# A gated mix of a long convolution and a shifted MLP: x added to the second product by accumulating DMAs, two small jobs moved, and a finer ranking of the planner's work

## Chip, cores and metric

The kernel runs on one core of a Trainium2 chip. The metric is the device time of the whole program in microseconds. The core's engines are TensorE (PE; its weight loads are PEld), VectorE (DVE), ScalarE (ACT), GpSimd (POOL) and SyncE (SP). Here POOL mostly issues DMAs, among them all DMAs that add to their destination; SP issues plain DMAs and transposing ones.

## What is computed

S = 2048 tokens of D = 640, bfloat16; the MLP has F = 1536. The reference, cut to what matters:

```python
def A(q, k, v, shift_k, ssm_k, ssm_D):
    k_shift = sum(k_pad[:, t:t + S, :] * shift_k[:, 3 - t] for t in range(4))
    kv = k_shift * v
    y = irfft(rfft(kv, 2 * S) * rfft(ssm_k, 2 * S))[:S]      # long causal convolution
    return q * (y + kv * ssm_D)

def B(x, w1, w2, w3, w4):
    h = gelu(layernorm(x) @ w1)
    hs = shift_quarters(h, (+1, -1, +2, -2)) @ w2            # token shifts by quarter of D
    x1 = x + hs
    return x1 + gelu(layernorm(x1) @ w3) @ w4

x = A_q
g = sigmoid((x * gate_w).sum(-1))
out = g * A(x, ...) + (1 - g) * B(x, ...)
```

## The kernel before

**Tiles.** Token s = 1024 c + 8 p + rho sits on partition p, in one of 2 halves c and 8 rows rho. X (bfloat16, all 16 tiles of 128 x 640) holds x, then x1, then the output. XT holds the transposed layernorm, HT the first product's result, KV the product of shifted k and v. Five slots s0 to s4 of 5120 elements a partition, and two more in the taps' place, hold the transforms.

**MLP.** First layernorm by rows (0), (1), (2, 3), (4, 5), (6, 7): statistics on VectorE (`ln_bn`) or, for row 1, on ScalarE; the inverse root on POOL (L661); the scaling on VectorE (L705); transposes on TensorE (L718). First product (L794) in 4 stages of two rows; its results go through gelu to HT. HT has two pad columns, set to zero at L779, which overlay the row with the shift taps that TensorE reads at L589. 32 columns of each quarter go through `w1t`, a copy of parts of w1 that POOL makes (L565). Second product (L840) in 4 groups of two rows, two halves each, so 16 products, and each of them adds x by one more matmul with the identity per half (L843); ScalarE evicts the sum back into X (L511, tag `x1`). The second layernorm takes its statistics on VectorE for groups 0 and 1 (`LN2_DVE`) and on ScalarE for groups 2 and 3, scales on VectorE and is transposed by DMAs on SP. The load of w3's second half waits for the last second product and the first transposes, the loads of w4 for those transposes. Third and fourth products (L883, L902) follow in 4 stages.

**Convolution.** The transform is cut into 4 units (two halves of D, two residues kap). A unit takes forward transforms of the taps h and of kv (L938), a butterfly of each (`bh`, `bk`), a window, a pointwise complex product and a fold, all of these by `tt` (L484) on VectorE; then come inverse transforms on TensorE (L1099). The pointwise product has two forms: `pointwise`, and `pointwise_dma`, in which two of the sums are accumulating DMAs on POOL (`accumulate`, L522, tags `pwa` and `pwb`). `PW_DMA` lists the units (half, kap) with the second form. Slot s4 is the temporary of every unit's butterflies, pointwise product and fold.

**Order.** The program is a list of nodes with costs and dependences. `schedule` and `_forward` place them one at a time: of all nodes that are ready, the one that can start first on its engine comes next, and among equals the one of higher rank. Ranks are looked up by a node's tag, and the tag has its stage behind a colon (`mm2:4` is the second product's first group). The planner's clock decides nothing on the chip: there each engine runs its list in that fixed order and waits on semaphores. A dependence through memory follows from the order in which the nodes are written down; the second product is written down ahead of all units.

`MM2_DMA`, empty before, lists the groups of the second product in which x isn't added by matmuls: such a product is evicted to a staging place in slot s4 (four rows of it, used in turn), and when both halves of a row are there, `accumulate` adds them to X (tag `add2`). The mean of such rows is the mean of the product plus that of x (`ln_small`, L666).

Of the kernel before, what the change touches and what calls it, by code (L numbers as in the profile page):

```python
# [10 lines left out]
ACTF = mybir.ActivationFunctionType  # L11
# [68 lines left out]
class Prog:  # L80
# [66 lines left out]

    def schedule(self):

        for n in self.nodes:  # L150
            n.base = frozenset(n.deps)
            for d in n.deps:
                d.users.append(n)
        for n in reversed(self.nodes):
            tail = max((u.prio for u in n.users), default=0.0)
            n.prio = tail + (n.cost if n.kind == "c" else n.cost + 2.0 + n.bytes / self.RATE)
        for n in self.nodes:
            n.prio = self.PRIO.get(n.tag, n.prio)
        self._forward()

    def _forward(self):
# [10 lines left out]
        known_at = {}  # L172
        pair_free = [0.0] * PAIRS
        pair_job = [None] * PAIRS
        link = 1.6
        xlink = 0.0

        def move(at, nbytes):
# [20 lines left out]
        while left:  # L199
# [16 lines left out]
            n = best[1]  # L216
            e = n.eng
# [6 lines left out]
            elif n.kind == "dma" and e == "pool" and n.bytes < self.SMALL:  # L224
                link = move(link, n.bytes)
                n.end = t + 4.5
            elif n.kind == "dma":
                link = move(max(link, t), n.bytes)
# [132 lines left out]
def bass_gated_mix__ssm_conv_h3__mixer_s_mlp__prompt_kernel(  # L361
# [4 lines left out]
    LN1_XP = ()  # L366
    SUM_DMA = (0,)
    KV_DMA = ((1, 0), (1, 1))
    MM2_DMA = ()
    W_AFTER = True  # L370
    PW_NEG = ()
    BF_DMA = ()
    INV_SPLIT = ((1, 0), (1, 4))
    PW_DMA = ((0, 0), (0, 1), (1, 0))
    LN1_ROWS = ((0,), (1,), (2, 3), (4, 5), (6, 7))
    LN1_DVE, LN2_DVE = ((0,), (2, 3), (4, 5), (6, 7)), (0, 1)
    P = Prog(nc)
# [51 lines left out]
    w1t = V(oW12 + 3200, 640).rearrange("p (c f) -> p c f", c=5)  # L429
# [4 lines left out]
    GM = V(oGM, 4096).rearrange("p (a i r s k) -> p a i r s k", a=2, i=2, r=4, s=2)  # L434
# [9 lines left out]
    ident = V(oID, 128)  # L444
# [35 lines left out]
    def dve(fn, r, w, n, psum=False, tag="", **kw):  # L480
        return P.op("dve", lambda e, ps: fn(e), r=r, w=w, cost=c_dve(n, psum), tag=tag, **kw)
# [4 lines left out]
    def act(o, i, func, n, scale=None, bias=None, acc=None, tag="", group=None, job=None, accgroup=None):  # L486
        r = [x for x in (i, scale, bias) if x is not None and not isinstance(x, float)]
        kw = {}
        if scale is not None:
            kw["scale"] = scale  # L490
        if bias is not None:
            kw["bias"] = bias
        if acc is not None:
            kw["accum_out"] = acc
        naps = sum(1 for x in (scale, bias) if x is not None and not isinstance(x, float))
        node = P.op("act", lambda e, ps: e.activation(o, i, func, **kw), r=r, w=[o], cost=c_act(n, naps, acc is not None),  # L496
                    tag=tag, group=group)
        if acc is not None:
            P._track(node, [], [acc], accgroup)
        return node  # L500
# [58 lines left out]
    for c in range(2):  # L559
# [2 lines left out]
    load_halo(0)  # L562
    load_k(0, 0)
    w1s, w1d = w1v.rearrange("p c (g f) -> p c g f", g=4)[:, :, :, 128:160], w1t.rearrange("p c (g f) -> p c g f", g=4)
    P.op("pool", lambda e, ps: e.tensor_copy(w1d, w1s), r=[w1s], w=[w1d], cost=1.2, tag="w1t")  # L565
    load_k(0, 1)
    load_x("sp", 0, 4, 8)
    load_x("sp", 1, 4, 8)
# [3 lines left out]
          w=[GWT], nbytes=100000, after=[late], tag="gw")  # L572
# [184 lines left out]
    v0, r0, nm0 = [stat(0, f)[:, :, 0:2] for f in ("var", "rs", "nm")]  # L757
# [18 lines left out]
    SHIFT = [1, -1, 2, -2]  # L776
    for col in (0, 257):
        z = HT[:, 0:4, :, col:col + 1]
        dve(lambda e, z=z: e.memset(z, 0.0), [], [z], 32, group="pad")  # L779
    for j, d0 in enumerate(SHIFT):  # L780
        rs = slice(0, d0) if d0 > 0 else slice(8 + d0, 8)
        col = 1 if d0 > 0 else 256
        z = HT[32 * j:32 * j + 32, 4, rs, col:col + 1]
        dve(lambda e, z=z: e.memset(z, 0.0), [], [z], 2, group="tail")
    RAW = [V(oGM + 512 * i, 512) for i in range(2)]
    for sc in range(4):
        P.stage = sc
        for fp in range(3):
# [13 lines left out]
            else:  # L802
                raw = RAW[sc % 2]
                evict(job, raw, lambda ps: bank(ps, 0, 512), ACTF.Gelu_apprx_tanh, 512, tag="gelu1t")
                for j, d0 in enumerate(SHIFT):
# [4 lines left out]
                    for carry, lst in todo.items():  # L810
                        k0, rho0, n = lst[0][0], lst[0][1], len(lst)
# [275 lines left out]
    def inverse(half, slot0, slot1):  # L1087
# [50 lines left out]
    inverse(1, "s3", "k0")  # L1138

    P.PRIO = {  # L1140
# [25 lines left out]
    }  # L1166
    P.schedule()
    P.assign_waits()
# [30 lines left out]
```

## Time and profile before

| | us |
|---|---|
| three runs, median (lowest to highest) | 244.91 (243.86 to 245.47) |
| profiled execution | 245.85 |
| its span, first to last instruction | 244.1 |
| mean granted TensorE clock | 0.987 |

The span lies inside the profiled execution's time. Busy times in microseconds, by stretches of the span:

```profile
core 0: us, PE busy (x) PEld busy (x) DVE busy (x) ACT busy (x) POOL busy (x), PEclk, DMA share, GB/s
0.00:20.00 20.00, 9.82 (x42) 4.67 (x43) 15.15 (x60) 10.05 (x17) 6.59 (x14) 1.00 0.93 335
20.00:40.00 20.00, 19.84 (x178) 12.98 (x180) 18.57 (x35) 17.35 (x18) 7.47 (x12) 1.00 1.03 358
40.00:60.00 20.00, 19.95 (x209) 13.71 (x209) 17.69 (x17) 14.23 (x21) 8.48 (x13) 0.91 0.63 154
60.00:80.00 20.00, 20.00 (x149) 14.43 (x148) 19.90 (x39) 13.14 (x25) 3.39 (x3) 1.00 0.41 74
80.00:100.00 20.00, 19.95 (x135) 13.15 (x135) 14.60 (x25) 19.51 (x35) 2.86 (x4) 1.00 0.75 165
```

PEclk is the granted share of TensorE's clock, and the DMA share is that of the core's 16 DMA engines. A busy time counts overlapping instructions once; a group's mean duration contains the overlap with its neighbours. In the chain of waits each line is a start, a length and what the end of the program depended on there.

### The profile page before, as it was taken

The numbers are of one execution on the slowest core, as the hardware profiler recorded it, in microseconds if no ns is written. First come the engines' busy times: TensorE is split into PE (matmuls) and PEld (weight loads), VectorE is DVE, ScalarE is ACT, GpSimd is POOL, SyncE is SP. The second block draws the span as 40 slices with busy tenths as digits, with TensorE's granted clock in tenths as the row PEclk, the third lists the DMA queues.
The fourth block names the chain that finished last, engine by engine and source line by source line (L and its number), as shares of the span: only waits on it lengthen the run. The fifth ranks groups of instructions, "written<-read, shape, count | busy, mean of one in ns | idle before, by whom it ended". The sixth has DMA issues, their size and how long they took to land.

```text
span 244.1 us, 3961 instructions
## 1 busy us (share of the span) xinstructions
PE 223.6 (92%) x1557; PEld 142.4 (58%) x1569; DVE 215.7 (88%) x337; ACT 154.3 (63%) x236; POOL 57.9 (24%) x70
## 2 busy tenths in 40 slices
PE   0579999999999999969999999999999998999990
PEld 0236576577777775525677645577546773777760
DVE  4899989996999758998989699799994899999992
ACT  5536899647468999956997456652257224127881
POOL 5311452451013040145002121001220011015910
PEclk9999999979999999999999999999999999999997
DMA  6999998098019649665585325403248034934998
GB/s 217 369 398 331 397 362 301 22 246 156 3 19 191 88 113 293 141 129 107 106 104 183 56 51 77 85 3 54 53 56 110 0 55 70 382 88 74 160 214 253
DMA packets 29938, 37.32 MB, mean 153 GB/s; under 512 B 12464, under 2 KB 22960, under 8 KB 29792
## 3 DMA queue, kind: packets, MB, share of 16 engines
q0 software_dynamic: 9424, 15.21, 32.0%
q1 hardware_dynamic: 20496, 21.86, 29.7%
q8 instruction: 12, 0.20, 0.3%
q14 instruction: 6, 0.05, 0.1%
HBM read 21.79 MB, written 2.62 MB: 100 GB/s over the span
## 4 chain that ended last, share of the span: by engine, by line
PE 88%; DMA 5%; DVE 3%; ACT 1%; issue 1%; SPq 0%; ACTq 0%
PE PS L902 21%; PE PS L883 18%; PE PS L938 14%; PE PS L794 10%; PE PS L840 9%; PE PS L1099 7%; DMA arena<-in_B_w_dram 3%; PE PS L641 3%; PE PS L718 2%; PE PS L843 2%; DMA arena<-in_A_q_dram 1%; DVE arena L686 1%; ACT arena L511 1%; PE PS L752 1%; DVE arena L705 1%
## 5 line engine op out<-in xcount | busy, mean ns | idle before, releaser
L484 DVE TENSOR_TENSOR arena<-arena 128x1280 bf16<-128x1280 bf16 (+2 forms) x192 | 180.3, 999 | 12.3 <-ACT arena L511 9.9
L511 ACT ACTIVATE arena<-PS 128x640 bf16<-128x640 f32 (+3 forms) x129 | 96.6, 821 | 42.5 <-PE PS L883 21.9
L522 POOL DMA_DIRECT2D arena<-arena x26 | 29.4, 1207 | 106.3 <-ACT arena L511 64.8
L883 PE MATMUL PS<-arena 128*128 128x512 bf16 x232 | 51.9, 379 | 2.4 <-DMA arena<-in_B_w_dram 2.0
L902 PE MATMUL PS<-arena 128*128 128x320 bf16 x384 | 52.8, 299 | 1.1 <-ACT arena L511 1.1
L511 ACT ACTIVATE arena<-PS,arena 128x320 bf16<-128x320 f32 (+1 forms) x48 | 27.6, 615 | 36.9 <-PE PS L902 34.2
L902 PEld LDWEIGHTS PS<-arena 128*128 128x128 bf16 x384 | 37.5, 98 | 16.1 <-ACT arena L511 1.6
L883 PEld LDWEIGHTS PS<-arena 128*128 128x128 bf16 x240 | 23.3, 98 | 29.6 <-DMA arena<-in_B_w_dram 2.5
L938 PE MATMUL PS<-arena 128*128 128x320 bf16 x256 | 36.4, 299 | 0.0
L938 PEld LDWEIGHTS PS<-arena 128*128 128x128 bf16 x256 | 25.1, 98 | 10.6
L840 PE MATMUL PS<-arena 128*128 128x320 bf16 x160 | 27.6, 310 | 0.0
L794 PE MATMUL PS<-arena 128*128 128x512 bf16 x96 | 23.8, 404 | 1.6 <-ACT arena L511 1.4
L686 DVE BATCH_NORM_STATS2 arena<-arena 128x6 f32<-128x320 bf16 x44 | 19.0, 467 | 4.9 <-DMA arena<-in_A_q_dram 2.5
L496 ACT ACTIVATE arena<-arena 128x640 bf16<-128x640 bf16 (+2 forms) x30 | 21.8, 756 | 1.7 <-DMA arena<-in_A_q_dram 1.7
L840 PEld LDWEIGHTS PS<-arena 128*128 128x128 bf16 x160 | 16.1, 101 | 6.8
L794 PEld LDWEIGHTS PS<-arena 128*128 128x128 bf16 x100 | 10.0, 103 | 13.6 <-issue 4.4
L1099 PE MATMUL PS<-arena 128*128 128x320 bf16 x128 | 17.6, 299 | 0.0
L1099 PEld LDWEIGHTS PS<-arena 128*128 128x128 bf16 x128 | 12.5, 98 | 4.9
L661 POOL TENSOR_TENSOR arena<-arena 128x4 f32<-128x4 f32 (+1 forms) x9 | 10.1, 1118 | 16.7 <-DVE arena L691 11.4
L705 DVE TENSOR_SCALAR arena<-arena 128x640 bf16<-128x640 bf16 x32 | 12.4, 440 | 1.3 <-issue 1.2
L822 POOL DMA_DIRECT2D arena<-arena x18 | 9.7, 544 | 8.5 <-ACT arena L511 8.5
L645 ACT ACTIVATE arena<-PS 128x1280 bf16<-128x1280 bf16 x8 | 9.5, 1263 | 2.4 <-PE PS L641 2.4
(43 smaller groups left out, 73.3 us busy)
## 6 DMA issues: line engine op xcount, KB each, us to landing
arena<-arena POOLq DMA_DIRECT2D x7, 640.0 KB, 5.6
arena<-in_A_q_dram SPq DMA_DIRECT2D x6, 640.0 KB, 8.0
arena<-in_B_w_dram POOLq DMA_DIRECT2D x4, 960.0 KB, 7.7
arena<-arena POOLq DMA_DIRECT2D x11, 320.0 KB, 3.7
arena<-in_A_ssm_k_dram SPq DMA_DIRECT2D x5, 512.0 KB, 11.4
arena<-in_A_k_dram SPq DMA_DIRECT2D x4, 640.0 KB, 17.1
arena<-in_A_v_dram SPq DMA_DIRECT2D x4, 640.0 KB, 20.5
out_dram<-arena SPq DMA_DIRECT2D x16, 160.0 KB, 2.1
```

Of the source, the lines that this page charges most:

```text
L484: return dve(lambda e: e.tensor_tensor(o, a, b, op), [a, b], [o], n, tag=tag, **kw)
L496: node = P.op("act", lambda e, ps: e.activation(o, i, func, **kw), r=r, w=[o], cost=c_act(n, naps, acc is not None), tag=tag, group=group)
L511: node = P.op("act", lambda e, ps: e.activation(ov, inner(ps), func, **kw), r=r, w=[o], cost=c_act(n, len(r), acc is not None), job=job, t ...
L522: P.dma("pool", lambda e, ps: e.dma_start(o, i, accum_op=ALU.add, max_dma_last_dim=2560), r=[o, i], w=[o], nbytes=3 * 256 * n, cost=1.2, t ...
L686: dve(lambda e, o=o, x=x: e.bn_stats(o, x), [x], [o], 640, tag="bn", group=("bn", l, rho, c))
L705: P.op("dve", lambda e, ps, b=b, x=x, rs=rs, nb=nb: e.tensor_scalar(b, x, rs, nb, op0=ALU.mult, op1=ALU.add), r=[x, rs, nb], w=[b], cost=0 ...
L794: fns.append(lambda e, ps, b=b, c=c, lhsT=lhsT, sc=sc: e.matmul(bank(ps, b, 512), lhsT, XT[:, c, 2 * sc:2 * sc + 2, :], start=(c == 0), st ...
L840: fns.append(lambda e, ps, hh=hh, ft=ft, lhsT=lhsT, last=by_dma and ft == 4: e.matmul(bank(ps, hh, 320), lhsT, w2v[:, ft, 320 * hh:320 * h ...
L883: fns.append(lambda e, ps, b=b, ft=ft, c=c, sc=sc: e.matmul(bank(ps, b, 512), w3v[ft // 6][:, c, 128 * (ft % 6):128 * (ft % 6) + 128], XT[ ...
L902: fns.append(lambda e, ps, hh=hh, ft=ft, lhsT=lhsT: e.matmul(bank(ps, hh, 320), lhsT, w4v[:, ft, 320 * hh:320 * hh + 320], start=(ft == 0) ...
L938: fns.append(lambda e, ps, r=r, ri=ri, s=s, b=b, rhs=rhs: e.matmul(bank(ps, b, 320), FM[:, kap, r, s, ri, :], rhs, start=(s == 0), stop=(s ...
L1099: fns.append(lambda e, ps, kap=kap, ri=ri, c=c, r=r, s=s: e.matmul(bank(ps, c, 320), GM[:, kap, ri, r, s, :], Qs[kap][:, r, ri, c, :], sta ...
```

## The change

- `MM2_DMA` names all four groups: the 32 matmuls with the identity are left out, the 16 products go to the staging place in slot s4, and 8 accumulating DMAs on POOL add them to X, one per row.
- `PW_DMA` gets the last unit (1, 1), whose pointwise product so takes the form with two accumulating DMAs.
- The copy to `w1t` moves from POOL to ScalarE.
- The memsets of the pads get a tag of their own, so that they can be ranked; they stay on VectorE.
- Tags with several nodes are cut into up to four parts (`mm2:4` becomes `mm2:4.0` to `mm2:4.3`), and the table of ranks is a new one with a rank for each part.
- The planner's start value for the DMA link goes from 1.6 to 0.8.

```diff
+        parts = {}
         for n in self.nodes:
-            n.prio = self.PRIO.get(n.tag, n.prio)
+            parts.setdefault(n.tag, []).append(n)
+        for tag, ns in parts.items():
+            for i, n in enumerate(ns):
+                if len(ns) > 1:
+                    n.tag = f"{tag}.{i * min(len(ns), 4) // len(ns)}"
+                n.prio = self.PRIO.get(n.tag, self.PRIO.get(tag, n.prio))
...
-        link = 1.6
+        link = 0.8
...
-    MM2_DMA = ()
+    MM2_DMA = (0, 1, 2, 3)
...
-    PW_DMA = ((0, 0), (0, 1), (1, 0))
+    PW_DMA = ((0, 0), (0, 1), (1, 0), (1, 1))
...
-    P.op("pool", lambda e, ps: e.tensor_copy(w1d, w1s), r=[w1s], w=[w1d], cost=1.2, tag="w1t")
+    act(w1d, w1s, ACTF.Copy, 640, tag="w1t")
...
-        dve(lambda e, z=z: e.memset(z, 0.0), [], [z], 32, group="pad")
+        dve(lambda e, z=z: e.memset(z, 0.0), [], [z], 32, group="pad", tag="pad")
...
-        dve(lambda e, z=z: e.memset(z, 0.0), [], [z], 2, group="tail")
+        dve(lambda e, z=z: e.memset(z, 0.0), [], [z], 2, group="tail", tag="pad")
...
     P.PRIO = {
...
+        "mm2:5.2": 296, "mm2:6.1": 294, "mm2:7.0": 292, "fwdh:0.3": 269, "mm2:4.2": 264, "mm2:7.1": 242,
+        "mm2:6.2": 240, "fwdh:1.2": 182, "mm2:5.3": 181, "fwdh:1.0": 179, "fwdh:0.0": 177, "mm2:4.3": 177,
+        "mm2:7.2": 177, "mm2:4.0": 159, "mm2:5.1": 159, "fwdh:1.3": 159, "fwdh:1.1": 155, "mm2:4.1": 145,
+        "fwdh:0.1": 119, "mm2:7.3": 117, "mm2:5.0": 116, "mm2:6.0": 115, "fwdh:2.0": 113, "mm2:6.3": 112,
+        "fwdh:0.2": 96, "xn:0.1": 108, "xn:0.0": 59, "pad.0": 40,
...
     }
```

The ranks shown are those of the second product, of the taps' transforms in units 0 to 2 and of the pads; the rest of the table is left out.

113 rows, old and new, of the table final are left out of this document.

## The prediction

> **What bounds the kernel now.** I read the busy shares first, then the engines by stretch, then the chain of waits in order of time, then groups by shape and VectorE's timeline. Busy shares, as busy us (share of the span) xinstructions:
>
> ```profile
> PE 223.6 (92%) x1557; PEld 142.4 (58%) x1569; DVE 215.7 (88%) x337; ACT 154.3 (63%) x236; POOL 57.9 (24%) x70
> ```
>
> Two engines are nearly full. The stretches show that it is the same ones all the way:
>
> ```profile
> core 0: us, PE busy (x) PEld busy (x) DVE busy (x) ACT busy (x) POOL busy (x), PEclk, DMA share, GB/s
> 126.00:190.00 64.00, 63.79 (x393) 38.58 (x395) 56.68 (x61) 35.21 (x46) 9.42 (x9) 1.00 0.40 72
> 190.00:223.00 33.00, 31.83 (x223) 21.60 (x223) 32.53 (x36) 9.98 (x14) 3.45 (x4) 1.00 0.40 112
> ```
>
> TensorE has no room in the first, VectorE none in the second. So a gain on TensorE alone moves the end only as far as VectorE follows. The chain (start us, us, what):
>
> ```profile
> 8.57 0.07 DVE arena L662
> 8.63 1.14 issue
> 9.78 0.15 DVE arena L705
> ...
> 10.57 0.59 DVE arena L662
> ...
> 15.05 6.45 PE PS L794 x20
> ...
> 73.04 0.68 PE PS L840 x5
> 73.72 0.14 PE PS L843
> ...
> 99.94 8.15 DMA arena<-in_B_w_dram
> ...
> 205.86 1.03 ACT arena L511
> ```
>
> To be seen: a start on VectorE with a hole of 1.14 us; then TensorE, where each half of a second product is five matmuls in 0.68 us (0.136 each) and one more in 0.14, the one that adds x; a load behind which TensorE stood 2.0 us at 106.1; a wait of 1.1 us at 205.8. Shapes, as busy us, mean ns | idle before:
>
> ```profile
> L484 DVE TENSOR_TENSOR arena<-arena 128x2560 bf16<-128x2560 bf16 x65 | 94.1, 1486 | 2.5 <-ACT arena L511 2.3
> L484 DVE TENSOR_TENSOR arena<-arena 128x1280 bf16<-128x1280 bf16 x101 | 78.0, 821 | 9.2 <-ACT arena L511 7.3 <-DMA arena<-arena 1.4
> L843 PE MATMUL PS<-arena 128*128 128x320 bf16 x32 | 9.8, 306 | 0.0
> ```
>
> The means overlap: start to start the VectorE ones are 1.41 and 0.74 us in the timeline, and L843 0.137. VectorE's timeline, and the accumulating DMAs of L522 (duration ns of the issue, then landing):
>
> ```profile
> 59.02 10.04 DVE L484 TENSOR_TENSOR arena<-arena 128x2560 bf16<-128x2560 bf16 x9 [2.27 <-ACT arena L511]
> 93.33 7.55 DVE L484 TENSOR_TENSOR arena<-arena 128x1280 bf16<-128x1280 bf16 x8 [0.99 <-ACT arena L511]
> 189.82 2.30 DVE L484 TENSOR_TENSOR arena<-arena 128x1280 bf16<-128x1280 bf16 x3 [3.67 <-ACT arena L511]
> DMA to landing us min/median/max: 3.3/4.4/7.2
> ```
>
> By the emitted order, unit 0's butterfly of h (six operations, 5.8 us by pitch) lies in the first, its window and butterfly of k (1.6 and 5.9) in the second, and its pointwise starts at 100.9.
>
> **Term 1, x by DMA: TensorE.** 32 matmuls of L843 go: 32 x 0.137 = 4.4 us (the page's chain gives this kernel's L843 2% of the span). All of it is on the chain. The same x1 evictions stay (0.70 us each).
>
> **Term 2, what x by DMA adds.** Eight accumulations of 320 KB on POOL: 8 x 1.2 = 9.8 us of a queue that is busy 3.4 of 20 us from 60 to 80, and 3.7 us from issue to landing by the 320 KB row. Behind them wait the second layernorm, its transposes, and with these the loads of w3's second half and of w4, all later in their row's chain by some 4.6 us. Cover: VectorE has the rest of k*v, TensorE the forward transforms (128 matmuls, 17.4 us). Product, transforms and half clock end near 90; the first half of w3 then covers 6.4 us. The load behind which TensorE stands now needs the last product (near 81 below) and the first transposes, so with 8.15 us it lands by 90: the 2.0 us stall goes. If that cover fails, 2.0 us stay. The Trainium skill, SBUF — State Buffer, section Who interferes with whom, says that a DMA issued from POOL cannot get its descriptors written while VectorE runs a two-port operation such as tensor_scalar, though tensor_tensor does not do this. The layernorm's four tensor_scalars in a row (0.36 us pitch) would by it hold one issue 1.5 us, and the forecast would be up to 1.5 us higher; the issues here (0.86 to 1.69 us) lie beside tensor_tensor and don't show it.
>
> **Term 3, the staging place.** The sums are staged in slot s4, which is also the temporary of every butterfly. Now unit 0's butterfly of h runs at 59 to 66, among the second products. With the change it has to wait until the last accumulation has read s4: call that R. First product at 50.4 (less the start's gain, 1.2) = 49.2; 16 x 1.36 = 21.8; the stretch at half clock now costs 1.4; so 72.4 with nothing between, and eviction 0.7 plus issue and landing 3.8 make R = 77. Each transform put before the last product adds its time, at most 17.4: R = 94.4. The new ranks place unit 2's transforms of h behind the products (they also need all of unit 0's and 1's, whose lowest rank is 96, against 112 for the lowest product), so I take the 64 matmuls of units 0 and 1 (8.7 us): R = 86. The butterflies of h and k then follow, 11.7 us: pointwise at 97.7 against 100.9, a gain of 3.2 that has the start's in it. VectorE has enough to do until R: from 24.4 to 100.9 it works 67.1 us (76.5 less 9.4 idle), without the butterflies 55.4, so it is done by 78 and idles about 8 us, as now.
>
> **Term 4, the start.** The two pads (L779) stand ahead of the first row's L705 and wait for the shift taps' matmuls, which end at 9.66: 1.15 us idle, 0.2 for the pads. At 10.49 an L662 takes 0.67 us beside POOL's copy of w1 (10.42, 0.72 us); its kind has 0.15. Removed: up to 1.9 us. The copy on ScalarE is one more ACTIVATE of 640 (0.79) in front of, at worst, the first row's eviction (1.24); the second row's then ends near 13.7 in place of 14.9. I take 1.2, ends 0 and 1.9. The pads stay on VectorE; only rank moves them.
>
> **Term 5, last unit.** Pointwise goes from six 2560s and eight 1280s to five and seven: 1.41 + 0.74 = 2.15 us off VectorE. Added: two accumulations, the larger 640 KB. In unit 2 that one started 8.9 us after its pointwise did and by its row lands 5.6 later, 7.2 at worst: 14.5 to 16.1, while VectorE has 11.7 of pointwise and 1.5 of fold. A wait of 1.3 to 2.9, into which inverse 0's multiplications (0.41 pitch, seven there now) can go. Net between 0 and 2.15 gained; I take 1.5, as units 0 to 2 show one wait on a DMA, 1.38.
>
> **Term 6, ranks by quarters, link.** They add no work; they decide who goes first. After 101 VectorE idles 9.5 us in all, 6.4 in three waits for evicted transforms (0.73, 1.96, 3.67). Bounds: 9.5 gained, or as much again lost; I take 1.5, part of the 3.67, where the window (1.6 us) needs only that its transforms come sooner.
>
> **Sum.** TensorE's path: 1.2 + 4.4 + 2.0 + 1.1 (205.8) = 8.7. VectorE's: 3.2 + 1.5 + 1.5 = 6.2. The smaller counts: 6.2. The profiled execution took 245.85 (span 244.1 and 1.75 around it): 239.65. It stands 0.94 above the median 244.91, where the same gain gives 238.7.
>
> **Rivals.** *A, both paths give way* (8.7): 236.2. For it: the waits left on VectorE mostly end on transforms, which come earlier. Against: 190 to 223 shows VectorE full. Chance 0.12.
>
> *B, VectorE keeps the end.* TensorE's 4.4 turns into waits, the staging eats what the ranks give, only the start is seen: 243.7. For it: VectorE's 88%. Against: it loses 2.15 us itself. Chance 0.15. If even the pads stay ahead, the change fails to do what it says there and this becomes 244.4.
>
> *C, slower: the staging place comes free too late.* If the last products stay behind all 128 transforms and the 19 matmuls of w3 (4.3 us) that precede them now, R = 98.7; pointwise starts at 110.4, 9.5 late; less 1.5 and 1.5, +6.5: 251.4. It decides from R = 92.2 (100.9 + 3.0 - 11.7). For it: that is the order of now, the last product ending at 99.65. Against: the ranks. Chance 0.13.
>
> **How the numbers follow.** Forecast 0.60, A 0.12, B 0.15, C 0.13. One per cent, about what a measurement here tells from no change, is 242.5 to 247.4. The forecast's own range is 236.5 to 242 (R from 80 to 89, term 5's ends). The range leaves out C and a tip of A: 235.3 to 244.3. Faster: 0.58 of the forecast + 0.12 of A + 0.03 of B = 0.73. Same: 0.02 of the forecast + 0.11 of B + 0.01 of C = 0.14. Slower: 0.01 of B + 0.12 of C = 0.13.
>
> **What would show it.** No L843; TensorE's first L794 near 13.8; no wait for w3; the last x accumulation landing near 86 and VectorE's first 2560 butterfly there; pointwise of unit 0 near 98; the last fold some 6 us sooner. It is wrong if TensorE shows new holes between 60 and 110, or if VectorE idles over 10 us before R.

## The result and the profile after

| us | median (lowest to highest), runs | ratio to before, 95% |
|---|---|---|
| before | 243.82 (241.4 to 245.47), 14 | |
| after | 246.19 (244.02 to 247.93), 14 | 1.0107 (1.0072 to 1.0143) |

The change makes the kernel about 1% slower; forecast were 238.7 and a gain. Medians and ranges, here and below, are of all runs, while the ratios leave out slow ones (over 1.5% above the kernel's fastest), without which the medians are 246.06 for after and, of the variants below, 244.76 for start_order, 241.44 for w4_late, 241.40 for both_orders and 238.58 for both_orders_half. The profiled executions mislead if they are set side by side: that of before (245.85, span 244.1) is slower than all 14 runs, that of after (244.88, span 243.1) the second fastest, and by them alone the change gains 1 us. So the lines below are read for what happens inside the program, and a second profile of each kernel stands beside them further on.

The profile after, first the busy shares (busy us, share of the span, instructions):

```profile
PE 219.9 (90%) x1537; PEld 138.7 (57%) x1537; DVE 213.6 (88%) x335; ACT 155.0 (64%) x237; POOL 71.8 (30%) x79
```

TensorE lost 3.7 us of work and two points of its share: it waits more than before. VectorE lost 2.1 us, as many as term 5 takes off it. POOL gained 13.9 us. The stretches:

```profile
core 0: us, PE busy (x) PEld busy (x) DVE busy (x) ACT busy (x) POOL busy (x), PEclk, DMA share, GB/s
72.00:90.00 18.00, 16.59 (x125) 11.48 (x124) 12.94 (x37) 16.95 (x34) 5.85 (x6) 1.00 1.14 157
96.00:100.00 4.00, 0.18 (x2) 0.05 (x2) 4.00 (x6) 2.24 (x5) 0.00 (x0) 0.98 1.04 348
100.00:103.00 3.00, 3.00 (x8) 1.07 (x9) 3.00 (x6) 0.00 (x0) 1.31 (x1) 0.50 0.54 176
126.00:190.00 64.00, 64.00 (x403) 39.18 (x402) 60.16 (x65) 39.22 (x54) 9.47 (x9) 1.00 0.40 71
190.00:223.00 33.00, 31.88 (x224) 21.63 (x222) 30.41 (x34) 11.35 (x17) 7.84 (x8) 1.00 0.67 149
```

The first of these stretches in the profile of before:

```profile
72.00:90.00 18.00, 18.00 (x135) 12.94 (x134) 14.22 (x39) 17.12 (x30) 4.55 (x6) 1.00 0.71 115
```

From 72 to 90 the DMA engines are full: the share is 1.14, before 0.71. (It is the sum of the packets' times over 16 engines; it can pass 1 only where packets overlap on an engine.) From 96 to 100 TensorE stands, and from 100 to 103 it works at half its clock. In 190 to 223 VectorE, full in the profile of before, has 2.6 us to spare. The chain (start us, us, what):

```profile
4.57 1.67 DVE arena L693 x4
...
10.81 1.26 PE PS L725 x10
...
14.52 5.07 PE PS L801 x15
...
73.80 1.18 POOL arena L529
...
79.76 2.27 SPq L719
...
82.07 7.19 DMA arena<-arena
...
89.88 0.87 POOL arena L525
90.75 9.16 DMA arena<-in_B_w_dram
...
99.96 14.73 PE PS L890 x60
...
204.15 1.03 ACT arena L518
```

The lines of the functions have moved by 7: L801 is the first product, L847 the second, L890 the third, L945 the forward transforms, L712 the scaling, L719 the second layernorm's transposes, L525 the loads, L529 the accumulations, L491 VectorE's arithmetic. To be seen: at the start VectorE's hole of 1.14 us is gone, and the first product begins at 14.52, half a microsecond sooner; an accumulation of x (73.80) and a transpose that takes 7.19 us (82.07) have come into the chain; behind it starts the load of w3's second half (90.75), which lands at 99.91; the 60 matmuls that waited for it then take 14.73 us. The wait at 204.15 is the old one of 205.86. TensorE's timeline (start, length, line; in brackets the idle time before it and what ended it):

```profile
80.79 7.30 PE L945 MATMUL PS<-arena 128*128 128x320 bf16 x52
89.50 6.64 PE L890 MATMUL PS<-arena 128*128 128x512 bf16 x30 [1.41 <-ACT arena L518]
99.96 14.73 PE L890 MATMUL PS<-arena 128*128 128x512 bf16 x60 [3.82 <-DMA arena<-in_B_w_dram]
```

The two holes add up to 5.2 us. The profile of before has one, of 2.0:

```profile
108.14 6.65 PE L883 MATMUL PS<-arena 128*128 128x512 bf16 x29 [2.03 <-DMA arena<-in_B_w_dram]
```

The first hole of after is put down to an eviction, but TensorE goes on 0.24 us after the last of the first four transposes lands (89.26), which is what the third product reads. VectorE's shapes and timeline, then the landings of L529 and of L719 (two answers about their lines):

```profile
L491 DVE TENSOR_TENSOR arena<-arena 128x2560 bf16<-128x2560 bf16 x64 | 92.3, 1482 | 3.8 <-DMA arena<-arena 3.7
L491 DVE TENSOR_TENSOR arena<-arena 128x1280 bf16<-128x1280 bf16 x100 | 76.8, 819 | 6.0 <-ACT arena L518 4.6 <-DMA arena<-arena 0.9
```

```profile
89.28 0.45 DVE L712 TENSOR_SCALAR arena<-arena 128x640 bf16<-128x640 bf16 x1 [3.13 <-DMA arena<-arena]
89.65 8.82 DVE L491 TENSOR_TENSOR arena<-arena 128x2560 bf16<-128x2560 bf16 x9
127.99 3.63 DVE L491 TENSOR_TENSOR arena<-arena 128x1280 bf16<-128x1280 bf16 x3 [3.95 <-ACT arena L518]
```

```profile
DMA to landing us min/median/max: 3.4/5.0/7.7
```

```profile
DMA to landing us min/median/max: 2.6/3.8/12.0
```

One operation of each size went. VectorE stands 3.13 us ahead of a scaling whose buffer a slow transpose is still reading, and 3.95 us ahead of a window whose transforms TensorE, late by then, has yet to do. The accumulations' median of 5.0 was 4.4; the transposes' median was 3.0 and their longest 6.3.

**Where the time went.** Issue to landing, in us, of the DMAs that decide, read from the trace's records (`xT:4` are the four transposes of the first second-layernorm group, in their order; `add2` the last two accumulations of x):

| kernel | last two `add2` | `xT:4` | w3's second half: issued, landed | took |
|---|---|---|---|---|
| before | none | 4.48, 3.66, 3.19, 2.66 | 99.94, 108.09 | 8.15 |
| after | 4.91, 6.42 | 4.87, 4.05, 5.80, 7.19 | 90.75, 99.91 | 9.16 |

The accumulations were issued at 80.05 and 82.26, the third and fourth transposes at 79.76 and 82.07. POOL stands from 83.5 to 89.9, until the transposes have landed, and then issues three of 960 KB each within 1.8 us: w4, w3's second half, w4.

### The profile page after: what moved, and what is told of

It is laid out like the page before. It is cut to its first block, busy times and chain, and to the rows that moved or that the text cites. A ratio compares the mean times of both kernels' runs of the same rounds, so it can differ in the third digit from the quotient of the medians.

```text
span 243.1 us, 3923 instructions
## 1 busy us (share of the span) xinstructions
PE 219.9 (90%) x1537; PEld 138.7 (57%) x1537; DVE 213.6 (88%) x335; ACT 155.0 (64%) x237; POOL 71.8 (30%) x79
## 4 chain that ended last, share of the span: by engine, by line
PE 80%; DMA 8%; DVE 4%; ACT 2%; POOL 1%; SPq 1%; issue 1%; ACTq 0%; POOLq 0%
PE PS L909 22%; PE PS L890 19%; PE PS L801 10%; PE PS L945 9%; PE PS L847 8%; PE PS L1106 7%; DMA arena<-in_B_w_dram 4%; DMA arena<-arena 3%; PE PS L648 2%; DVE arena L693 2%; ACT arena L518 2%; PE PS L725 2%; DMA arena<-in_A_q_dram 1%; SPq L719 1%; DVE arena L712 1%; PE PS L759 1%
## 5 line engine op out<-in xcount | busy, mean ns | idle before, releaser
L491 DVE TENSOR_TENSOR arena<-arena 128x1280 bf16<-128x1280 bf16 (+3 forms) x190 | 177.9, 995 | 12.7 <-ACT arena L518 7.0
L529 POOL DMA_DIRECT2D arena<-arena x36 | 41.9, 1201 | 106.9 <-ACT arena L518 57.8
L890 PE MATMUL PS<-arena 128*128 128x512 bf16 x240 | 54.7, 387 | 5.2 <-DMA arena<-in_B_w_dram 3.8
L909 PE MATMUL PS<-arena 128*128 128x320 bf16 x384 | 53.5, 299 | 1.1 <-ACT arena L518 1.1
L890 PEld LDWEIGHTS PS<-arena 128*128 128x128 bf16 x240 | 23.7, 99 | 34.2 <-DMA arena<-in_B_w_dram 4.3
L945 PE MATMUL PS<-arena 128*128 128x320 bf16 x256 | 37.0, 299 | 0.0
L945 PEld LDWEIGHTS PS<-arena 128*128 128x128 bf16 x256 | 24.8, 98 | 10.5 <-issue 0.2
L801 PE MATMUL PS<-arena 128*128 128x512 bf16 x100 | 24.2, 399 | 1.4 <-ACT arena L518 1.4
L847 PE MATMUL PS<-arena 128*128 128x320 bf16 x160 | 23.3, 299 | 0.0
L847 PEld LDWEIGHTS PS<-arena 128*128 128x128 bf16 x160 | 15.4, 98 | 6.1 <-DMA arena<-arena 0.3
L668 POOL TENSOR_TENSOR arena<-arena 128x4 f32<-128x4 f32 (+1 forms) x9 | 12.9, 1428 | 17.9 <-DVE arena L681 10.9
L1106 PE MATMUL PS<-arena 128*128 128x320 bf16 x128 | 17.7, 299 | 0.0
L801 PEld LDWEIGHTS PS<-arena 128*128 128x128 bf16 x100 | 9.9, 102 | 13.3 <-issue 2.2
L712 DVE TENSOR_SCALAR arena<-arena 128x640 bf16<-128x640 bf16 x32 | 12.6, 437 | 3.2 <-DMA arena<-arena 3.1
L829 POOL DMA_DIRECT2D arena<-arena x18 | 9.9, 556 | 14.0 <-ACT arena L518 13.9
L725 PE MATMUL PS<-arena 128*128 128x128 bf16 x80 | 6.2, 242 | 5.9 <-DVE arena L669 5.9
```

The lines of the kernel that those rows point to most:

```text
L491: return dve(lambda e: e.tensor_tensor(o, a, b, op), [a, b], [o], n, tag=tag, **kw)
L529: P.dma("pool", lambda e, ps: e.dma_start(o, i, accum_op=ALU.add, max_dma_last_dim=2560), r=[o, i], w=[o], nbytes=3 * 256 * n, cost=1.2, t ...
L712: P.op("dve", lambda e, ps, b=b, x=x, rs=rs, nb=nb: e.tensor_scalar(b, x, rs, nb, op0=ALU.mult, op1=ALU.add), r=[x, rs, nb], w=[b], cost=0 ...
L801: fns.append(lambda e, ps, b=b, c=c, lhsT=lhsT, sc=sc: e.matmul(bank(ps, b, 512), lhsT, XT[:, c, 2 * sc:2 * sc + 2, :], start=(c == 0), st ...
L847: fns.append(lambda e, ps, hh=hh, ft=ft, lhsT=lhsT, last=by_dma and ft == 4: e.matmul(bank(ps, hh, 320), lhsT, w2v[:, ft, 320 * hh:320 * h ...
L890: fns.append(lambda e, ps, b=b, ft=ft, c=c, sc=sc: e.matmul(bank(ps, b, 512), w3v[ft // 6][:, c, 128 * (ft % 6):128 * (ft % 6) + 128], XT[ ...
```

## The experiments

The theory: TensorE still sets the end. It is rid of the matmuls that add x, but the accumulations take the DMA engines just when the first transposes need them; these land late, the load of w3's second half starts late and beside two other loads, and TensorE stands twice and then runs at half clock. Rivals: the order of the three loads alone does it; VectorE, the last unit's accumulations or the start do it; the traffic can't be avoided and only hits another transfer when one is moved out of its way.

In all variants of the changed kernel the order of instructions that the planner made is kept, written out as a list for each engine, and only the edit shown is made in it (TensorE's lines are then 82 or 83 higher than after). In the lists of POOL and of the others below, `add2:6` are the accumulations of x in the third group of the second product, the last two in time, `ln:n` a layernorm's step, `w31` and `w4` the loads of w3's second half and of w4.

**1 and 2. Both kernels once more, unaltered.**

> The changed kernel once more, nothing altered, for a second profile: the first one (244.88 us) is among the shortest of the changed kernel's runs, whose median is 246.19. Theory 1 (late load): TensorE again stands about 3.8 us at 96 behind the load of w3's second half and then has one stretch of 3.4 us at half clock; a longer run shows a longer stall there or a second such stretch. Theory 2 (VectorE or DMA contention everywhere): the stall at 96 is the same or shorter and the run's extra time lies in other holes, after 130.

> The kernel before once more, nothing altered: its first profile (245.85 us) is longer than its median of 243.82. Both theories expect a span of 242 to 244; the question is which waits are shorter than in the first profile. Theory 1: TensorE's 2.0 us behind the load of w3's second half is the part that varies, 0 to 2 us. Theory 2: differences are spread over VectorE's holes.

246.28 and 244.0, each near its median. TensorE's account by the four profiles, and by three of the variants below (idle is that after its first L801). Time is also lost at half clock, in two places. At the start a matmul of L801 takes 0.43 us, and 0.22 from the time in the column "full clock" on; half of what lies between is lost. Later, a window of 3.41 us at half clock loses 1.7:

| profile | first L801 (L794) | full clock, lost before it | TensorE's end | from first to end | idle | half clock later, at | work left |
|---|---|---|---|---|---|---|---|
| before | 15.05 | 19.09, 2.0 | 237.54 | 222.49 | 2.03 + 1.11 | 1.7, 49.8 | 215.6 |
| before_again | 14.38 | 19.86, 2.7 | 235.42 | 221.04 | 1.11 | 1.7, 50.6 | 215.5 |
| after | 14.52 | 17.91, 1.7 | 236.01 | 221.49 | 1.41 + 3.82 + 1.12 | 1.7, 99.8 | 211.7 |
| after_again | 16.07 | 19.46, 1.7 | 237.14 | 221.07 | 1.48 + 3.58 + 1.11 | 1.7, 101.4 | 211.5 |
| x_by_matmul | 14.15 | 19.57, 2.7 | 234.27 | 220.12 | 0.38 + 1.12 | none | 215.9 |
| both_orders_half | 13.77 | 19.58, 2.9 | 231.45 | 217.68 | 1.12 | none | 213.7 |
| w4_late | 14.24 | 18.83, 2.3 | 231.55 | 217.31 | 1.93 + 1.12 | none | 212.0 |

The holes of after come back in after_again, so they belong to the kernel. What makes after_again longer is not a longer stall or a second window, which the theory expected of a longer run, but a later start. The 2.03 us of before don't come back, so that wait is there in some runs only. The start varies by 1.5 us with one order: in after the load of half of row 2 lands at 6.65, in after_again at 8.47, and the statistics of that row stand on VectorE ahead of row 0's scaling. When the full clock comes doesn't follow the start: in the fourteen profiles it is 16.7 to 20.2, 2.7 to 5.8 us after the first L801.

**3. The load of w3's second half freed of its wait for the transposes,** and put on POOL ahead of the last accumulation.

```diff
-             after=turned[4] if hf and W_AFTER else ())
+             after=())
 POOL:
-  ln:4 add2:6 ln:5 add2:6 w4 w31 w4 ln:6
+  ln:4 add2:6 ln:5 w31 add2:6 w4 w4 ln:6
```

> The changed kernel with its order of instructions kept, except that the load of w3's second half no longer waits for the first transposes and is issued on POOL right after the second root of group 5, near 82 in place of 90.75. Theory 1: it lands by 91, TensorE's wait at 96 (3.8) and the half clock behind it (1.8 lost) go, VectorE's hole at 124 (3.95) goes with them: 3.5 to 5.6 us less than the changed kernel, about 241 to 242.5 and a ratio to before of 0.985 to 0.995. Theory 2: the 960 KB now run beside the last x accumulations and the first transposes, which land later by as much; TensorE stands before its first L890 instead, and the time is within 1.2 of the changed kernel.

246.57, ratio 1.0151 (1.0077 to 1.0225): nothing gained; the 241 to 242.5 of the theory were missed. TensorE's timeline:

```profile
80.23 7.30 PE L1028 MATMUL PS<-arena 128*128 128x320 bf16 x52
93.56 21.90 PE L973 MATMUL PS<-arena 128*128 128x512 bf16 x88 [6.03 <-DMA arena<-arena]
```

The load lands at 90.64, and the hole is still there, in one piece of 6.03 us: the fourth transpose, with an accumulation and the load beside it, now takes 11.65 us. The rival that traffic moved away hits the next transfer was right for this move.

**4. The load of w3's second half ahead of w4's on POOL.**

```diff
 POOL:
-  add2:6 w4 w31 w4 ln:6
+  add2:6 w31 w4 w4 ln:6
```

> The changed kernel with one swap in POOL's order: the load of w3's second half goes ahead of the first load of w4, both still behind the first transposes. Theory 1: issued 0.9 us earlier and with less beside it, it lands 1 to 2.5 us earlier; the stall falls from 3.8 to between 1.3 and 2.8, the half clock stays or goes: 1 to 4 us less than the changed kernel (242 to 245). Theory 2: no more than 0.5 us.

242.91, 0.9985 (0.9942 to 1.0027): 3.3 below after (3.0 by the ratios), with intervals apart, and no longer slower than before. The load takes 7.65 us in place of 9.16, and TensorE's holes are 1.72, 1.43 and 1.89 with no half clock behind them. The third is new: the last transpose of the second group, beside the loads of w4, lands at 105.15.

**5. x by matmuls again, all else as in the changed kernel,** its order too.

```diff
-    MM2_DMA = (0, 1, 2, 3)
+    MM2_DMA = ()
```

> The changed kernel with its order kept, but x added by the 32 matmuls again (the eight x accumulations left out of POOL's order). Theory 1 (the x accumulations fill the DMA engines between 72 and 100, where their share is 1.06 against 0.80 before, and so make the transposes and the loads behind them late): TensorE has 4.4 us more, but the first transposes land in 2.7 to 4.5 us in place of 4.9 to 7.2, the loads are issued 4 to 9 us earlier and TensorE's waits at 89 and 96 (1.4 and 3.8) and the half clock (1.8) go: within 1.5 us of the changed kernel, or faster. Theory 2 (the stall comes from the order of the loads alone, the accumulations are harmless): the same stall stays and the time is 3 to 5 us more than the changed kernel's, about 250.

241.94, 0.997 (0.9927 to 1.0013): 4.2 below after (3.3 by the ratios) although 4.4 us of matmuls come back, and not near 250. The stretch and TensorE's timeline:

```profile
72.00:90.00 18.00, 18.00 (x138) 12.79 (x137) 10.63 (x32) 15.59 (x31) 4.69 (x4) 1.00 0.35 67
```

```profile
85.89 7.30 PE L1027 MATMUL PS<-arena 128*128 128x320 bf16 x52
93.24 10.74 PE L972 MATMUL PS<-arena 128*128 128x512 bf16 x49
```

The DMA share is 0.35 in place of 1.14, the first four transposes take 2.64 to 2.69 us each, and TensorE goes from the transforms into the third product and on with one hole of 0.38 us at 104: w3's second half, still behind a load of w4, lands at 96.92. So the accumulations go with the holes. A part of that is only that TensorE, with its matmuls back, comes to the third product at 93.24 and not at 88.09. With the landings of this run (transposes 87.92, load 96.92) the TensorE of after would still have stood from 94.7 (88.09 and 30 matmuls) to 96.92, at most 2.2 us; the other 3.0 of its 5.2 come from transposes and a load that land later beside the accumulations. At 99.96, where after goes on behind its load, this kernel has done the same 30 matmuls (93.24 + 30 x 0.219 = 99.8): the holes had eaten all that the matmuls saved, and the half clock behind them put after 1.7 us behind (TensorE's end, 236.01 to 234.27). The rest of the change by itself, terms 4 to 6 in the order that was planned for the staging place, is worth 0.3%, with an interval that holds no change.

**6. The last unit's pointwise without accumulating DMAs,** so that its sums are VectorE's again.

```diff
-    PW_DMA = ((0, 0), (0, 1), (1, 0), (1, 1))
+    PW_DMA = ((0, 0), (0, 1), (1, 0))
```

> The changed kernel with its order kept, but the last unit's pointwise product all on VectorE again, without the two accumulating DMAs. If VectorE sets the end (the prediction's term 5): 1.5 to 2.2 us more than the changed kernel. If TensorE does, as its chain says (inverse transforms without a hole from 218.4 to 236.0): the last fold ends about 2 us later, at 231 to 232, which is still ahead of the inverse groups that need it or just at them: 0 to 1.5 more.

247.08, 1.0168 (1.009 to 1.0246): 0.9 above after, with intervals that overlap. The last unit's DMAs aren't what makes the change slow; whether they help isn't settled.

**7. Both loads of w4 behind the next layernorm step, at 102, and w3 ahead of them.**

```diff
 POOL:
-  add2:6 w4 w31 w4 ln:6 pwa:0
+  add2:6 w31 ln:6 w4 w4 pwa:0
```

> The changed kernel with three loads moved in POOL's order: w3's second half ahead of w4, and both halves of w4 behind the root of group 6 (101.7), some 11 us later. Theory 1 (DMA engines full between 72 and 106): w3's second half lands 7 us after its issue or sooner, near 98, the last transposes of group 5 at 95 to 98 in place of 103 to 105, so TensorE's waits of 1.4 to 3.8 at 97 and of 1.9 at 104 shrink to under 1.5 in all and no half clock follows: 1.5 to 2.5 us less than with the swap alone (242.9), about 240.5 to 241.5. Theory 2: w4, landing near 113, now meets the first unit's accumulating DMAs and costs VectorE there what TensorE gains: 242.5 or more.

241.86, 0.993 (0.9885 to 0.9975), 4.3 below after. TensorE:

```profile
88.36 6.42 PE L973 MATMUL PS<-arena 128*128 128x512 bf16 x29
96.71 13.12 PE L973 MATMUL PS<-arena 128*128 128x512 bf16 x59 [1.93 <-DMA arena<-in_B_w_dram]
```

One hole of 1.93 us, no half clock (59 matmuls in 13.12 us, after 60 in 14.73), and the second group of transposes, in the way before, lands by 97.70. The load still takes 8.54 us with no other load from POOL beside it; beside it are the second group's transposes. The time lies between the two expectations, nearer that of the theory.

**8. The start reordered:** the identity first on POOL, the copy to `w1t` behind the first rows' evictions, rows 0 and 1 scaled ahead of row 2's statistics.

```diff
 POOL:
-  drow w2t w2t w2t w2t ident ln:0
+  ident drow w2t w2t w2t w2t ln:0
 ScalarE:
-  shk w1t xTe:0 xTe:1 gelu1:0
+  shk xTe:0 xTe:1 w1t gelu1:0
 VectorE (bn: statistics, xn: scaling):
-  bn:2#3-5 bn:2#9 ln:0#3 ln:1#0 bn:2#10 ln:1#2 ln:1#1 bn:2#11 ln:1#3 xn:0 bn:2#0-1 ln:1#5 bn:2#2 xn:1
+  ln:0#3 xn:0 ln:1#0 ln:1#2 ln:1#1 ln:1#3 bn:2#3-5 ln:1#5 xn:1 bn:2#9-11 bn:2#0-2
```

> The changed kernel with only its first 13 us put in another order: the identity for the transposes first on POOL's queue, the first two rows' scaling on VectorE ahead of the statistics of later rows (which wait for a load that lands at 6.5 in some runs and 8.5 in others), the copy of w1 on ScalarE behind the two evictions. If the new order of the start is what cost the typical run its gain there: the first L801 starts near 13.3 in place of 14.5 to 16.1 and the time is 1 to 2.5 us less than the changed kernel, 243.7 to 245.2. Otherwise (the start is hidden behind the loads of later rows, or the stall at 96 absorbs it): under 0.7.

245.04, 1.0126 (1.002 to 1.0232): not told apart from after. The profile shows the start itself: L801 at 13.59, and 13.67 to 13.79 in the three kernels below that have it, where the eight profiles with the changed kernel's start lie between 14.07 and 16.07. But the full clock comes at 17.91, as in after, so of the 0.93 us by which TensorE starts sooner half is run at half clock.

**9, 10, 11. Both orders (7 and 8) together, with x all by DMA, all by matmul, and by DMA in the first two groups only.**

```diff
both_orders:        MM2_DMA = (0, 1, 2, 3)
both_orders_matmul: MM2_DMA = ()
both_orders_half:   MM2_DMA = (0, 1)
```

> The changed kernel with both order edits that helped: the three loads as in w4_late, the first 13 us as in start_order; x by accumulating DMAs. If the two gains add (3 to 4 us from the loads, 1.2 from the start): 240 to 241.5, a ratio to before of 0.985 to 0.993, and TensorE from its first L801 to its last matmul in 217 to 218 us. If the start is absorbed by the wait for w3's second half, which does not start earlier: 241.5 to 242.

> The same two order edits, x added by the 32 matmuls. This tells whether the accumulations cost by themselves or only by what they do to the loads. Theory 1 (they cost only through the full DMA engines beside the loads): with the loads moved, TensorE's 4.4 us count again, and this kernel takes 2 to 4 us more than both_orders, 242.5 to 244. Theory 3 (accumulations make the second layernorm so late that 4.4 us of TensorE are never worth it): this kernel takes the same time as both_orders or less, 240 to 241.5.

> The same two order edits, x by accumulating DMAs for groups 0 and 1 alone (rows 0 to 3), by matmuls for groups 2 and 3, whose accumulations (issued at 74 to 82) run beside the first transposes. TensorE's saving is 2.2 in place of 4.4. Theory 1: the first transposes land in 2.7 us again and w3's second half follows some 2 us sooner, so the wait that is left (1.9) goes: within 0.7 us of both_orders, 240 to 242. Theory 3: between the two others.

| | median | ratio, 95% | w3's second half | TensorE's holes, 80 to 110 |
|---|---|---|---|---|
| both_orders | 241.62 | 0.9929 (0.9886 to 0.9972) | 91.66 to 99.42 | 1.50, 1.55 |
| both_orders_matmul | 241.01 | 0.9913 (0.9876 to 0.995) | 88.19 to 94.32 | none |
| both_orders_half | 238.91 | 0.9817 (0.9755 to 0.9878) | 86.09 to 92.40 | none |

Here the theory missed. It let the accumulations cost only beside the loads, so that with the loads moved the matmuls would count again (both_orders_matmul at 242.5 to 244); yet all x by DMA and none can't be told apart (241.62, 241.01). The loads are not all of it: in both_orders the first four transposes still take 4.85, 4.01, 5.87 and 7.32 us. And both_orders_half, expected within 0.7 of both_orders or between the two others, is below both. Its stretch, and TensorE's timeline:

```profile
72.00:90.00 18.00, 18.00 (x138) 12.78 (x136) 13.71 (x38) 15.59 (x31) 4.16 (x3) 1.00 0.65 120
```

```profile
83.28 7.30 PE L1028 MATMUL PS<-arena 128*128 128x320 bf16 x52
90.41 19.59 PE L973 MATMUL PS<-arena 128*128 128x512 bf16 x90
```

Its four accumulations have landed by 70.53, eight us before the first transpose is issued (78.53); the first four take 4.24, 3.46, 2.98 and 2.67; the DMA share is 0.65, and the ninety matmuls of the third product follow the transforms without a gap. The first two groups are worth 2.1 us (241.01 to 238.91; 2.3 by the ratios), about what their 16 matmuls cost (16 x 0.137 = 2.2), though the two intervals just touch; the last two cost 2.7 (238.91 to 241.62), intervals apart, and would have saved 2.2 more. The start's gain isn't seen in run 9 against run 7, the second of its two expectations: TensorE there runs at half clock from 49.1 to 52.6 and has two holes of 1.5 us in place of one of 1.93.

**12. Only the last two groups by matmul, all else as in the changed kernel.**

```diff
-    MM2_DMA = (0, 1, 2, 3)
+    MM2_DMA = (0, 1)
```

> The changed kernel with its order kept (neither the loads nor the start moved) and one thing different: x by accumulating DMAs for groups 0 and 1 alone, by matmuls for groups 2 and 3. If the four late accumulations (rows 4 to 7, issued from 64 to 82) are what filled the DMA engines beside the transposes: the first transposes land within 3 to 4 us, TensorE's waits at 89 and 96 are gone or under 1.5 in all, and the time is some 2 us under x_by_matmul (241.9), 239.5 to 241. If the three loads together are enough to stall it: the wait before w3's second half stays at 2 us or more and the time is 242 to 245.

241.08, 0.9894 (0.9805 to 0.9982): 5.1 below after, with intervals apart, just past the expected times. The holes are 0.83 and 0.37. In the changed kernel's own order, then, the accumulations of the last two groups alone turn a gain of 1% into a loss of 1%.

## Why the prediction was wrong, by its steps

**Term 1, 4.4 us off TensorE: right.** In the table of run 2 the work left is 215.5 to 215.9 with x by matmul, 213.7 with 16 of the matmuls gone and 211.5 to 212.0 with all 32 gone: 1.8 to 2.2 and 3.5 to 4.4, of 2.2 and 4.4 forecast.

**Term 2, the step that failed.** "The load behind which TensorE stands now needs the last product (near 81 below) and the first transposes, so with 8.15 us it lands by 90: the 2.0 us stall goes. If that cover fails, 2.0 us stay." It landed at 99.91, and the stall became 5.2, with a half-clock window behind it. Four parts of the step were wrong. It let the load go with the last product, though it names the transposes too. Before, the product came last of the two (99.65, the transposes at 87.10); with the product at 81 the transposes do, and even at 87.10, with the 0.6 us that after takes from there to the issue and 8.15 of load, it lands near 96. The transposes were left at their old length, 2.7 to 4.5 us; beside accumulations they took 4.1 to 7.2, and landed at 89.26 although the first was issued 2.9 us sooner than before (77.03, 79.96), so the load was issued at 90.75. The load was taken at its old 8.15 us; with a load of w4 on either side it took 9.16. Of that the first half of w3 covered what the step gave it (6.64 us, 6.4 forecast). And "2.0 us stay" was taken for the worst case, when a DMA can land later than before as well as earlier. The accumulations were priced on POOL's queue (1.2 us each) and by their own latency, but not by what they take from the DMA engines. That price can be read from the profiles: the queue that POOL issues on, in the page's list of DMA queues (packets, MB, share of 16 engines' span), with x by DMA

```profile
q0 software_dynamic: 13168, 18.82, 42.3%
```

and by matmul (run 5)

```profile
q0 software_dynamic: 10992, 16.19, 35.7%
```

The first is 102.8 us of all 16 engines (0.423 x 243.1), the second 85.8 (0.357 x 240.4): 17 us for eight accumulations, 2.1 each (of packets' time, which also holds what a packet waits beside another). The two that lie beside the third and fourth transposes so take 4 us of engines out of some 9.5 (79.76 to 89.26). The Trainium skill, DMA: Bandwidth & Descriptors, section Queues, rings and completion order, says that each DMA engine takes packets in turn from all queues that have work; that fits a transpose which takes twice its time and more as soon as POOL's queue has work, but no run here shows the packets' order.

The hold of up to 1.5 us on an issue that the prediction names isn't tested here: the eight issues took 1.18 to 1.27 us, and none lay beside a scaling of the layernorm. Two sums of the prediction are off by little and change nothing: 8 x 1.2 is 9.6 and not 9.8, and VectorE's 24.4 + 55.4 is 79.8, or 78.6 with the start's gain, and not 78.

In the sum, TensorE's 8.7 us were 1.2 + 4.4 + 2.0 + 1.1. By the two first profiles it got 0.5 from the start, 0.3 from less half clock there, 3.9 from the matmuls, lost 3.2 to the holes, and got nothing at 205: 1.5. From its end to the program's it lost 0.6 (7.1 us, before 6.5), which leaves about the 1.0 by which the two spans differ. Between before_again and after_again, the two near their medians, the same terms are -1.7 + 1.0 + 4.0 - 5.1 + 0 - 0.4: 2.2 slower, as their spans are.

**Term 3, the staging place: the place right, the gain not.** The last product ended near 80.7 (81.1 by the working of R), but the last accumulation landed at 88.68 where R was 86, as it took 6.4 us in place of the 3.7; the first 2560 butterfly came at 89.65 and the pointwise product of unit 0 at 101.6, not 97.7. Rival C's 98.7 for R didn't come, nor its loss of 6.5.

**Term 4, the start: mis-sized.** It was 1.2 us with ends of 0 and 1.9. Eight profiles of this start give 14.07 to 16.07 (14.52 in after) against 15.05 and 14.38: nothing that stands out. The new ranks put the identity last of POOL's first loads (landed at 10.76, in the two of before at 5.90 and 7.21), row 2's statistics ahead of row 0's scaling, and the copy of w1 ahead of the first eviction on ScalarE. The 13.8 that the prediction named was reached by reordering just these. What the step also left out is the clock: TensorE begins at half clock whenever it begins, and the full clock came between 16.7 and 20.2 regardless, so a microsecond at the start is worth as little as half of that.

**Terms 5 and 6** can't be told from nothing: together with term 4 they are run 5's 0.3%. The last unit's accumulation took 6.8 us and landed at 222.0, and VectorE's holes in front of it are 2.4 us (1.3 to 2.9 by the working); its last fold ended at 230.0, before at 232.9, but the fold isn't what ends last.

**Which path sets the end.** The prediction let the smaller gain count, VectorE's 6.2. TensorE's path was the one that counted: VectorE's largest new hole (3.95 us at 124) is a wait for it, and in both_orders_half, where TensorE is freed, VectorE follows to 238.91. Rival B (243.7, VectorE keeps the end) came nearest in time, for a reason that wasn't so; the direction was rival C's, for another reason. The rivals had one late resource, the staging place; that full DMA engines would delay the transposes and the load behind them was none of them, though the prediction did name new holes between 60 and 110 as what would prove it wrong.

**Open.** Whether the last unit's accumulations and the reordered start are worth anything in time; how the 5.1 us of run 12 divide among transposes, load and half clock; why the stretch from TensorE's last matmul to the program's last instruction is 7.0 to 7.9 us in the eight profiles with all x by DMA and 6.0 to 6.8 in the six others; and the order in which the DMA engines serve the queues.

## What to carry to other kernels

Work that is moved from an engine to a DMA is paid in the DMA engines' time, so look at the DMA share in the stretch where it lands, and at what else is in flight there: accumulations saved about the full 0.137 us per matmul where the engines had room, and cost more than they saved beside the transposes that the next product needs. Price a transfer's delay at the end of the chain that it starts (transposes, then a load held on the same queue, then the matmuls, then their clock), and let that term be negative. Where a queue holds several loads behind one wait, put the one that is needed first in front, and keep the others back: here the first alone was worth 3.3 us and both together 4.3, about as much as the matmuls saved. And when a change moves one of two conditions of a wait forward, look up the other: it now comes last.

## What the runs showed of the hardware

- A DMA transpose of 2.65 us took 4.1 to 7.2 beside the last accumulations of 320 KB, and 11.65 with a 960 KB load as well. Such an accumulation takes 2.1 us of packets' time on all 16 DMA engines. Loads do it too: beside the three loads of 960 KB in run 5, without accumulations of x, the second group's transposes took 6.5 to 10.3.
- After 3.6 to 4.2 us without work TensorE ran 3.41 us at half clock, with a hole of 6.03 us the half clock lasted 6.83; holes of up to 2.0 us had none behind them. The Trainium skill, TensorE: Matmul & The Clock Gate, section Part 1: The HAM clock gate, gives a free-running window of 3.4 us and two speeds only, and the traces agree (granted 0.50 in one row above, 1.00 in the others but for a window's edge).
- At the start TensorE ran at half clock from its first L801 (0.43 us a matmul, later 0.22) until 16.7 to 20.2, in every profile.
- The half clock near 50, behind 80 one-column matmuls of some 2 us, comes and goes between kernels whose TensorE does the same there: these matmuls begin at 46.90 in after, with no half clock, and at 46.91 in both_orders, with one from 49.1 to 52.6. By a window that runs free of the program the two could differ so; that wasn't tried.
- A load at the start landed at 6.65 in one execution and at 8.47 in another of the same kernel, and moved the first product by 1.55 us.
